# Seven half-size products in place of eight in the gated part, with wo converted early and q split as high, low, high

## The chip, the cores and the metric

The kernel runs on one core of a Trainium2 chip. The metric is device time in microseconds, from the runs of the whole kernel. TensorE (PE) multiplies into PSUM, ScalarE (ACT), VectorE (DVE) and GpSimd (POOL) do the elementwise work, and all DMAs are issued from SyncE's queue (SP).

## What is computed

Attention over 2 batches, 8 heads, 576 positions, head size 64, in which each row keeps its 32 largest scores; then a layer of four experts; then a gated layer, whose weights arrive as 64-bit floats. Cut to what matters:

```
attn = softmax(top32(q k^T / 8)) v              # (2,8,576,64) -> x (1152, 512)
for e in range(4):                              # D 512, F 1024
    out += p[:, e:e+1] * (relu(x @ w1[e]) @ w2[e])
x = out
a = x @ w_a                                     # 512 -> 1536
b = x @ w_b                                     # 512 -> 1536
return (a * b) @ w_out                          # 1536 -> 512
```

## The kernel before

Every product of the two layers is made of three matmuls: each 32-bit operand is kept as a high and a low part in the format fp32r, and high x high, high x low and low x high are added in PSUM. The 1152 tokens are nine tiles of 128, in groups of 1, 2, 3 and 3 tiles (`SIZES`). Group after group goes through attention and then through `experts` (`plain` for the first group, of one tile); a group's result is turned by TensorE and split into the high and low parts of `xs` in `replace`. The last stage is `gated`.

No order is written by hand. Each instruction, or short run of them, is added to a `Plan` with its engine, an expected duration (`dve`, `act`, `pool_`, `mm_r`), a key, what it waits for and the buffers it uses. `Plan.order` plays the engines forward in time with those durations and at each moment gives each engine the ready operation with the smallest key; `Plan.best` tries 42 variants and emits the best. The instructions then sit on each engine's queue in that fixed order. Operations marked `port=True` (DVE work from SBUF to SBUF) are not started in the plan while POOL works: `ok = not (op.port and free.get("POOL", 0.0) > now)`. Buffers are slots in regions of SBUF that are used again by later stages (`again`); a slot can be taken once all earlier users of its words are through. The names of the regions (`big`, `mid`, `low`, `raw`, `ys`) are the names that the trace shows.

The gated part runs over six steps of 256 of the 1536 inner columns. Each step converts 256 rows or columns of w_a, w_b and w_out in `d_unit` (two parts each of 512 KB of 64-bit data, 36 parts in all): per part one load, three ACT operations and seven DVE operations, which rebuild a 32-bit value and a remainder from the 64 bits and end in a high and a low part in `wd` (region `big`, five slots). Then for each half of 128 columns and each block of 384 tokens, `first` makes a and b (12 matmuls of 384 columns each, 4 pieces of the 512 times 3), ACT copies a out of PSUM, DVE multiplies it by b, ACT and DVE split the product into high and low (L1158, L1161, L1164, L1167). `second` multiplies with w_out: nine token tiles, six matmuls of 512 columns each, and DVE adds the result to `res` (L1179). `first`, `second` and `replace` of the early groups share three PSUM banks (`ms`); all matmuls have one line, L459, in `mm`, and all transposes L462.

Around it: `w_unit` loads and splits the experts' weights, the low part on POOL early and on DVE late (L894); `keys` and `start_pair` load and split k and q (L514 on ACT, L518 on POOL, L516 on DVE for the first pair); `masked` finds the top 32 on DVE (L728 MAX8, L736 MATCH_REPLACE).

## Time and profile before

| | us |
|---|---|
| runs of the whole kernel, median of 3 (lowest, highest) | 841.27 (840.20, 841.86) |
| the profiled execution's own time | 840.31 |
| its span, first to last instruction | 838.5 |
| PE busy | 809.1 |
| DVE busy | 702.3 |
| ACT busy | 535.8 |
| POOL busy | 266.4 |
| mean granted TensorE clock over the span | 0.984 |

Busy time is the union of an engine's instructions. Matmuls are pipelined: one of 384 columns shows a duration of 335 ns, but the next starts long before it ends, so the cost of one in a row is read from start to start. The 1.8 us between the span and the profiled time lie outside the instructions.

### The profile page before, as it was taken

How to read it: one execution, taken by the hardware profiler on the slowest of the kernel's cores; microseconds unless marked ns; L12 is line 12 of the kernel's file. 1: busy time of each engine (PE TensorE's matmuls, PEld its weight loads, DVE VectorE, ACT ScalarE, POOL GpSimd, SP SyncE). 2: the span in 40 equal slices, each digit the busy share in tenths (PEclk: the TensorE clock that was granted, in tenths of full speed). 3: DMA queues.
4: the chain of work that ended last, by engine and by line, in shares of the span. 5: the costliest groups of instructions: out<-in, count | busy, mean ns of one | idle time of the engine just before them, and what ended most of it. 6: DMA issues, size and time to landing. Idle time of an engine off the chain costs nothing.

```text
span 838.5 us, 13976 instructions
## 1 busy us (share of the span) xinstructions
PE 809.1 (96%) x5141; PEld 726.0 (87%) x5141; DVE 702.3 (84%) x1363; ACT 535.8 (64%) x965; POOL 266.4 (32%) x249
## 2 busy tenths in 40 slices
PE   7689999999999999999999999999999999999997
PEld 5477787889988899999999998999898989999896
DVE  7999999999999989999969998545235889899724
ACT  6888887999899798897756556343125535344220
POOL 4534433899898947764210000000000000000000
PEclk8699999999999999999999999999999999999999
DMA  6849967746644635432335657343002222323003
GB/s 185 278 132 299 331 216 232 235 137 204 203 137 153 184 115 153 130 104 99 101 124 178 201 161 217 125 126 101 1 1 64 88 77 74 101 79 98 26 1 113
DMA packets 83540, 117.05 MB, mean 140 GB/s; under 512 B 10640, under 2 KB 54672, under 8 KB 83472
## 3 DMA queue, kind: packets, MB, share of 16 engines
q1 hardware_dynamic: 83472, 116.17, 44.2%
q8 instruction: 40, 0.66, 0.3%
q14 instruction: 28, 0.23, 0.1%
HBM read 109.07 MB, written 7.08 MB: 139 GB/s over the span
## 4 chain that ended last, share of the span: by engine, by line
PE 64%; DVE 29%; ACT 3%; issue 2%; DMA 1%; POOL 1%; SPq 0%; POOLq 0%; ACTq 0%; DVEq 0%
PE ps L459 62%; DVE low L728 14%; DVE low L736 11%; PE ps L462 3%; DVE mid L967 1%; DVE ys L992 1%; DMA raw<-in_moe_w_dram 1%; ACT low L778 1%; ACT low L707 0%; ACT low L767 0%; ACT big L656 0%; POOL low L763 0%; DMA low<-in_q_dram 0%; DVE xs L872 0%; ACT mid L893 0%
## 5 line engine op out<-in xcount | busy, mean ns | idle before, releaser
L728 DVE MAX8 low<-low 128x8 f32<-128x576 f32 x288 | 204.4, 747 | 3.9 <-ACT low L707 3.6
L459 PE MATMUL ps<-xs,mid 128*128 128x384 f32 (+1 forms) x1152 | 203.3, 320 | 0.9 <-DVE mid L967 0.5
L459 PE MATMUL ps<-mid 128*128 128x512 f32 x768 | 198.1, 394 | 0.2
L459 PEld LDWEIGHTS ps<-xs,mid 128*128 128x128 f32 x1152 | 185.4, 189 | 9.9 <-DVE mid L967 0.9
L736 DVE MATCH_REPLACE8 low<-low 128x576 f32<-128x576 f32 x216 | 159.3, 743 | 0.0
L459 PEld LDWEIGHTS ps<-mid 128*128 128x128 f32 x768 | 139.7, 188 | 22.3 <-DVE mid L967 0.6
L459 PE MATMUL ps<-xs,big 128*128 128x384 f32 x864 | 152.3, 335 | 0.0
L459 PEld LDWEIGHTS ps<-xs,big 128*128 128x128 f32 x864 | 150.1, 188 | 1.3 <-DVE xs L1028 0.3
L893 ACT ACTIVATE mid<-raw 128x1024 fp32r<-128x1024 f32 x96 | 102.2, 1069 | 39.1 <-PE ps L459 29.2
L894 POOL TENSOR_TENSOR mid<-raw,mid 128x1024 fp32r<-128x1024 f32 x48 | 115.0, 2406 | 12.2 <-ACT mid L893 10.9
L763 POOL TENSOR_TENSOR low<-low 128x576 f32<-128x576 f32 x70 | 99.9, 1443 | 27.2 <-ACT low L759 26.8
L894 DVE TENSOR_TENSOR mid<-raw,mid 128x1024 fp32r<-128x1024 f32 x48 | 58.6, 1220 | 25.4 <-ACT mid L893 25.0
L963 ACT ACTIVATE mid<-ps 128x384 fp32r<-128x384 f32 (+1 forms) x96 | 44.2, 464 | 52.2 <-PE ps L459 49.3
L459 PE MATMUL ps<-big,mid 128*128 128x512 f32 x324 | 76.0, 391 | 0.0
L459 PEld LDWEIGHTS ps<-big,mid 128*128 128x128 f32 x324 | 60.4, 188 | 12.8 <-DVE low L1179 0.6
L967 DVE SCALAR_TENSOR_TENSOR mid<-ps,mid 128x384 fp32r<-128x384 f32 (+1 forms) x96 | 48.0, 504 | 23.8 <-ACT mid L963 23.4
L1158 ACT ACTIVATE low<-ps 128x384 f32<-128x384 f32 x36 | 17.7, 493 | 71.6 <-PE ps L459 71.4
L778 ACT ACTIVATE low<-low 128x576 f32<-128x576 f32 x70 | 51.5, 781 | 15.3 <-DVE low L775 15.2
L759 ACT ACTIVATE low<-low 128x576 f32<-128x576 f32 x70 | 52.5, 781 | 10.2 <-POOL low L753 10.1
L767 ACT ACTIVATE low<-low 128x576 f32<-128x576 f32 x70 | 54.9, 785 | 2.1 <-POOL low L763 2.1
L707 ACT ACTIVATE low<-ps 128x576 f32<-128x576 f32 x72 | 47.2, 660 | 9.7 <-POOL low L763 6.2
L462 PE MATMUL ps<-identr,low 128*128 128x128 f32 x324 | 47.3, 282 | 5.5 <-ACT low L778 4.4
(88 smaller groups left out, 1009.8 us busy)
## 6 DMA issues: line engine op xcount, KB each, us to landing
raw<-in_moe_w_dram SPq DMA_DIRECT2D x122, 512.0 KB, 3.7
big<-kscr SPq DMA_DIRECT2D x20, 576.0 KB, 5.5
low<-in_v_dram SPq DMA_DIRECT2D x24, 256.0 KB, 3.1
low<-in_moe_w_a_dram SPq DMA_DIRECT2D x12, 512.0 KB, 4.4
low<-in_moe_w_b_dram SPq DMA_DIRECT2D x12, 512.0 KB, 3.8
low<-in_moe_w_out_dram SPq DMA_DIRECT2D x12, 512.0 KB, 3.6
kscr<-big SPq DMA_DIRECT2D x8, 576.0 KB, 5.4
ys<-in_moe_w_dram SPq DMA_DIRECT2D x6, 512.0 KB, 5.6
```

The lines of the kernel that those rows point to most:

```text
L459: nc.tensor.matmul(out, l, r, **kw)
L462: nc.tensor.transpose(out, a, i)
L707: S, lambda: nc.scalar.activation(s.ap.rearrange("p (c n) -> p c n", c=2), at.ap[:, :, 0:HALF], AF.Copy),
L728: 62 + 1.04 * width, lambda at=at, cs=cs: nc.vector.max(m8v()[:, x, cs], at()), key + 0.02 * r, [done],
L736: lambda at=at, cs=cs: nc.vector.match_replace(out=src[1](), in_to_replace=m8v()[:, x, cs], in_values=at(), imm_value=LOW),
L759: S, lambda x=x, s=s: nc.scalar.activation(ev(x), s.ap, AF.Relu, bias=endv()[:, x, 1:2], scale=-STEEP),
L763: pool_(S), lambda x=x, s=s: nc.gpsimd.tensor_tensor(ev(x), s.ap, ev(x), op=ALU.subtract), ks, [a], [s, ep]
L767: lambda x=x: nc.scalar.activation(ev(x), ev(x), AF.Exp, bias=endv()[:, x, 0:1], scale=scale, accum_out=sums.ap[:, x:x + 1]),
L778: S, lambda x=x: nc.scalar.activation(ev(x), ev(x), AF.Copy, scale=sums.ap[:, x:x + 1]),
L893: hi = scalar(1024, lambda: nc.scalar.activation(u.ap[:, 0:1024], r.ap, AF.Copy), 500 + s, [ld], [u, r], sbuf=True)
L894: sub = lambda eng: eng.tensor_tensor(u.ap[:, 1024:2048], r.ap, u.ap[:, 0:1024], op=ALU.subtract)
L967: lambda h=h, p=p: nc.vector.scalar_tensor_tensor(h.ap[:, n:2 * n], p.ap[:, 0:n], 0.0, h.ap[:, 0:n], op0=ALU.max, op1=ALU.subtract),
```

## The change

**Strassen.** The two products of the gated part, x w_a and x w_b, are taken together as one product of a 2 x 2 block matrix x (two halves of the tokens, two halves of the 512) with a 2 x 2 block matrix (two halves of the 512; b and a). Seven products of half-size blocks replace eight, with sums of blocks as operands. The token halves are cut so that set 0 (`own` 0) pairs tokens 0 to 383 with 384 to 767, and set 1 (`own` 1) pairs 768 to 959 with 960 to 1151: a product has 384 columns in set 0 and 192 in set 1, and is made of 6 matmuls (2 pieces of the 256 times 3). `combine` takes the place of `replace` for the last two groups and also makes the sums of x (S1 to S4), in `xt`; for group 2 mostly on POOL, for the last group on DVE and ACT. `d_unit` now makes, for 128 inner columns, the full 32-bit values of w_b and w_a, the sums T1 to T4 of their halves, and high and low parts of all seven operands: 12 units in 3 slots of 3584 words (5 of 2048 before), behind 2 slots `vv` for the values before the split. `multiply` runs the seven products into six PSUM banks of their own (`pps`), builds the four blocks with one ACT copy and seven DVE additions from PSUM, multiplies a by b on POOL (two), splits on ACT (high) and POOL (low). `second` gets two banks of its own (`ns`).

**wo.** `narrow` converts w_out in six steps of 256 rows ahead of the gated part, with the same seven DVE operations per part as before, and writes the result to DRAM (`wscr`, 1 MB per step); `gated` loads it back, 1 MB per step, into one slot `uo`. Keys: `turn_of` gives two units, the six steps of w_out and the other ten units, in this order, keys from 1210 on, behind all weights of the experts.

**q.** q's block is stored as high, low, high (3 x 64) instead of high, high, low, low (4 x 64); the two transposes take columns 0 to 127 and 64 to 191. The sum of products is the same; the low part is now computed for 64 columns per tile and head instead of 128.

The regions are moved: `s` and `pt` get a region of their own, in which `xt` comes later; `ys` moves into `low`; `res` takes the space of the experts' raw weights.

```diff
+    wscr = dr.tile([F2 // 256, 128, 2048], F32, name="wscr")
...
-    qspls = big.slots("qspl", 1, 2 * 3 * 4 * D)
+    qspls = big.slots("qspl", 1, 2 * 3 * 3 * D)
...
-    wds = big.slots("wd", 5, 2048)
+    wds = big.slots("wd", 3, 2 * 7 * 256)
...
+    vvs = low.slots("vv", 2, 2048)
+    tps = [low.slots("tpa", 1, 4 * 384), low.slots("tpb", 2, 4 * 192)]
+    uos = mid.slots("uo", 1, 2048)
...
+    pps = banks("pp", [(i, i + 1) for i in range(6)], 2)
+    ns = banks("n", [(6, 7), (7, 8)], 2)
...
+    def split2(dst, src, m, key, after, tiles, eng):
...
+        sub = lambda e: e.tensor_tensor(dst()[:, :, 1], src(), dst()[:, :, 0], op=ALU.subtract)
...
-                        tr(p[:, i, lh], sqv()[:, j, i, lh].rearrange("p a d -> p (a d)"), identr)
+                        tr(p[:, i, lh], sqv()[:, j, i, lh:lh + 2].rearrange("p a d -> p (a d)"), identr)
...
+    sets = [(0, 384, 384), (768, 960, 192)]
...
+    def combine(c, y, yd):
+
+        own = c == len(GROUPS) - 1
...
+        def half(a):
...
+            s1 = vector(dve(n), lambda: nc.vector.tensor_tensor(tv(3), qv(), tv(1), op=ALU.add), K, f + [qo], [q_, tp])
+            s3 = pool(n, lambda e: e.tensor_tensor(tv(1), tv(1), tv(0), op=ALU.subtract), K, [s1], [tp])
+            s2 = pool(n, lambda e: e.tensor_tensor(tv(0), tv(3), tv(0), op=ALU.subtract), K, [s3], [tp])
+            if own:
+                s4 = vector(dve(n), lambda: nc.vector.tensor_tensor(tv(2), q_.ap[:, 0:n], tv(0), op=ALU.subtract), K, [s2], [q_, tp])
+            else:
+                s4 = pool(n, lambda e: e.tensor_tensor(tv(2), tv(2), tv(0), op=ALU.subtract), K, [s2], [tp])
...
+            h2 = scalar(3 * n, lambda: nc.scalar.activation(xv(0)[:, :, a], t3(), AF.Copy), K, [s4], [tp, xt], sbuf=True)
+            l2 = pool(3 * n, lambda e: e.tensor_tensor(xv(1)[:, :, a], t3(), xv(0)[:, :, a], op=ALU.subtract), K, [h2], [tp, xt])
...
+        for a in range(2):
+            half(a)
...
+    def turn_of():
+        taken.append(0)
+        return BASE + 10 * len(taken)
...
+    def narrow(f):
+
+        s = turn_of()
+        u, vv = wds.tile(), vvs.tile()
...
+                d, r, o4, o5, o7 = double(wo[r0:r0 + 128], s, t, vv, 1, False)
+                o8 = scalar(512, lambda: nc.scalar.activation(hi(), t(), AF.Copy), s, [o4], [vv, u], sbuf=True)
+                o9 = vector(dve(512), lambda: nc.vector.tensor_tensor(t(), t(), hi(), op=ALU.subtract), s, [o8, o5], [vv, u], port=True)
+                o10 = vector(dve(512), lambda: nc.vector.tensor_tensor(lo(), t(), r(), op=ALU.add), s, [o9, o7], [vv, d, u], port=True)
...
+        return load(lambda: wscr[f], lambda: u.ap[:, 0:2048].bitcast(F32), s, got, [u], 1 << 20)
...
+    def d_unit(f):
+
+        s = turn_of()
+        u, vv = wds.tile(), vvs.tile()
+        f0 = 2 * f * 128
...
+        for i, w in ((0, wb), (1, wa)):
+            src = w[:, f0:f0 + 256].rearrange("(a p) n -> p a n", p=128)
+            vs.append(double(src, s + 0.01 * i, lambda i=i: t(i), vv, 2, True))
...
+        t13 = vector(dve(512), lambda: nc.vector.tensor_tensor(
+            two(v(4, 2)), v(0).unsqueeze(1).to_broadcast([128, 2, 256]), two(v(1, 2)), op=ALU.subtract), s, vs, [vv], port=True)
+        t2 = vector(dve(256), lambda: nc.vector.tensor_tensor(v(6), v(2), v(4), op=ALU.subtract), s, [t13], [vv], port=True)
+        t4 = vector(dve(256), lambda: nc.vector.tensor_tensor(v(7), v(3), v(6), op=ALU.subtract), s, [t2], [vv], port=True)
+        got = []
+        for i, n, after in ((0, 3, vs), (3, 4, [t13, t4])):
+            hi = scalar(n * 256, lambda i=i, n=n: nc.scalar.activation(u.ap[:, i * 256:(i + n) * 256], v(i + 1, n), AF.Copy), s, after, [vv, u], sbuf=True)
+            got += [hi, vector(dve(n * 256), lambda i=i, n=n: nc.vector.tensor_tensor(
+                u.ap[:, (7 + i) * 256:(7 + i + n) * 256], v(i + 1, n), u.ap[:, i * 256:(i + n) * 256], op=ALU.subtract), s, [hi], [vv, u], port=True)]
...
+        units = [d_unit(f) for f in range(FRONT)]
+        kept_wo = [narrow(f) for f in range(F2 // 256)]
+        units += [d_unit(f) for f in range(FRONT, F2 // 128)]
...
+        def product(un, own, x, w_):
+            u, ud, uv = un
+            m = sets[own][2]
+            p = pps.tile()
+
+            def emit():
+                for a in range(2):
+                    for i, (l, r) in enumerate(((0, 0), (0, 1), (1, 0))):
+                        mm(p.ap[:, 0:m], uv(l, w_, a), operand(x, own, r, a), start=(a == 0 and i == 0), stop=(a == 1 and i == 2))
+
+            return p, tensor(6 * mm_r(m), emit, 1000 + nxt(), ud + xdone2[own], [p, u, late_x[0]])
+
+        def multiply(un, own, g):
+
+            m = sets[own][2]
...
+            p1, p6, p7, p5, p2, p3, p4 = [
+                product(un, own, x, w_)
+                for x, w_ in ((A11, B11), (S2, T2), (S3, T3), (S1, T1), (A12, B21), (S4, B22), (A22, T4))
+            ]
+            e1 = scalar(m, lambda: nc.scalar.activation(tv(0), p1[0].ap[:, 0:m], AF.Copy), K, [p1[1]], [p1[0], tp])
+            u2 = add(1, p6, 0, [e1])
+            u3 = add(2, p7, 1, [u2])
+            u4 = add(1, p5, 1, [u3])
+            c22 = add(3, p5, 2, [u3])
+            c11 = add(0, p2, 0, [u2])
+            c12 = add(1, p3, 1, [u4])
+            c21 = add(2, p4, 2, [c22])
+            g0 = mul(0, 0, 1, [c11, c12])
+            g1 = mul(1, 2, 3, [c21, g0])
+            cs = slice(sets[own][0], sets[own][0] + 2 * m)
+            hi = scalar(2 * m, lambda: nc.scalar.activation(g.ap[:, 0:n][:, cs], tv(0, 2), AF.Copy), K, [g0, g1], [g, tp], sbuf=True)
+            lo = gpsimd(pool_(2 * m), lambda: nc.gpsimd.tensor_tensor(
+                g.ap[:, n:2 * n][:, cs], tv(0, 2), g.ap[:, 0:n][:, cs], op=ALU.subtract), K, [hi], [g, tp])
+            return [hi, lo]
...
+            both = [(units[2 * f + part], gs_.tile()) for part in range(2)]
+            gd = {}
+            for own, part in ((0, 0), (0, 1), (1, 0), (1, 1)) if pending else ((0, 0), (1, 0), (0, 1), (1, 1)):
+                gd[own, part] = multiply(both[part][0], own, both[part][1])
+                if pending:
+                    pending.pop()()
...
+                p, o = second(gts, [un_o + (0,), un_o + (1,)], t * 128, (), ns.tile())
```

The sums of blocks in `d_unit` and `combine` are as shown; `double` holds the first six DVE operations and two ACT operations of the old `d_unit`, with one more DVE addition of the remainder for w_a and w_b.

## Rows read from the trace of the kernel before

**Rows 1.** The page: busy time by engine, then tenths in 40 slices.
```profile
PE 809.1 (96%) x5141; PEld 726.0 (87%) x5141; DVE 702.3 (84%) x1363; ACT 535.8 (64%) x965; POOL 266.4 (32%) x249
...
DVE  7999999999999989999969998545235889899724
...
PEclk8699999999999999999999999999999999999999
```

**Rows 2.** Chain that ended last, in order of time: start, length, what.
```profile
479.32 137.13 PE ps L459 x696
...
617.95 215.94 PE ps L459 x1139
```

**Rows 3.** Windows: length, then busy PE, PEld, DVE, ACT, POOL, clock, DMA.
```profile
50.00:440.00 390.00, 381.57 (x2874) 334.52 (x2874) 379.65 (x795) 332.40 (x608) 241.84 (x207) 1.00 0.55 175
...
440.00:607.90 167.90, 167.90 (x881) 152.83 (x876) 116.35 (x175) 78.44 (x118) 0.00 (x0) 1.00 0.45 139
607.90:821.40 213.50, 213.49 (x1147) 201.49 (x1147) 153.64 (x284) 85.12 (x158) 0.00 (x0) 1.00 0.20 60
```

**Rows 4.** Timeline of PE, gated part: start, length, instructions merged.
```profile
647.35 24.11 PE L459 MATMUL ps<-xs,big 128*128 128x384 f32 x138
671.29 0.86 PE L459 MATMUL ps<-big,mid 128*128 128x512 f32 x3
...
672.52 11.95 PE L459 MATMUL ps<-big,mid 128*128 128x512 f32 x51
684.31 15.96 PE L459 MATMUL ps<-xs,big 128*128 128x384 f32 x91
```

**Rows 5.** Timeline of PE, an experts' stretch with 256 columns.
```profile
229.73 1.58 PE L459 MATMUL ps<-xs,mid 128*128 128x256 f32 x12
231.15 0.86 PE L459 MATMUL ps<-mid 128*128 128x512 f32 x3
```

**Rows 6.** Timeline of PE, an attention stretch with transposes of 128 columns.
```profile
189.12 0.63 PE L462 MATMUL ps<-identr,big 128*128 128x128 f32 x6
189.58 0.59 PE L459 MATMUL ps<-xs,mid 128*128 128x256 f32 x3
```

**Rows 7.** Groups by line and shape: count, busy us, mean ns, idle before.
```profile
L894 POOL TENSOR_TENSOR mid<-raw,mid 128x1024 fp32r<-128x1024 f32 x48 | 115.0, 2406 | 12.2 <-ACT mid L893 10.9 <-POOL low L772 0.6 <-POOL big L518 0.3
...
L894 DVE TENSOR_TENSOR mid<-raw,mid 128x1024 fp32r<-128x1024 f32 x48 | 58.6, 1220 | 25.4 <-ACT mid L893 25.0 <-PE ps L459 0.4
...
L1179 DVE TENSOR_TENSOR low<-ps,low 128x512 f32<-128x512 f32 x45 | 30.1, 686 | 11.6 <-PE ps L459 11.4
...
L1120 DVE SCALAR_TENSOR_TENSOR low<-low 128x512 uint32<-128x512 uint32 x36 | 24.8, 689 | 0.8
...
L1161 DVE TENSOR_TENSOR low<-ps,low 128x384 f32<-128x384 f32 x36 | 20.0, 555 | 36.3 <-ACT low L1158 30.3 <-PE ps L459 3.4 <-PE ps L462 2.5
...
L1118 DVE TENSOR_SCALAR low<-low 128x512 uint32<-128x512 uint32 x36 | 15.3, 424 | 0.8
...
L967 DVE SCALAR_TENSOR_TENSOR mid<-ps,mid 128x256 fp32r<-128x256 f32 x32 | 12.9, 412 | 0.0
...
L518 POOL TENSOR_TENSOR big<-low,big 128x384 fp32r<-128x384 f32 x8 | 7.9, 1011 | 3.0 <-ACT big L514 1.8 <-DMA raw<-in_moe_w_dram 1.2
```

**Rows 8.** Timeline of DVE: two instructions that follow each other, merged.
```profile
498.36 1.01 DVE L967 SCALAR_TENSOR_TENSOR mid<-ps,mid 128x384 fp32r<-128x384 f32 x2
```

**Rows 9.** Timeline of POOL: the same two instructions at two places.
```profile
393.93 2.80 POOL L763 TENSOR_TENSOR low<-low 128x576 f32<-128x576 f32 x2 [0.89 <-ACT low L759]
...
409.06 3.45 POOL L763 TENSOR_TENSOR low<-low 128x576 f32<-128x576 f32 x2 [1.81 <-ACT low L759]
```

**Rows 10.** Timeline of DVE at the second of these places.
```profile
408.62 1.20 DVE L894 TENSOR_TENSOR mid<-raw,mid 128x1024 fp32r<-128x1024 f32 x1
```

**Rows 11.** Writes into the wd slots before the gated part: count, ns, first and last start.
```profile
L1129 DVE TENSOR_TENSOR big<-low x10: 680/683/693, 446.4 to 514.4; 128x512 fp32r<-128x512 f32 x10
```

**Rows 12.** DMA issues: line, count, KB each, us to landing.
```profile
kscr<-big SPq DMA_DIRECT2D x8, 576.0 KB, 5.4
```

More of the change, by code (lines that the diff above doesn't have):

```diff
@@ L40, in __init__ @@
         self.name, self.aps, self.region, self.spans = name, aps, region, spans
+        self.whole = False
         self.free = set(range(len(aps)))
@@ L65, in cells @@
         a, b = self.spans[i]
-        return [(o.name, j) for o in self.beside for j, (c, d) in enumerate(o.spans) if c < b and a < d]
+        return [(o.name, j) for o in self.beside for j, (c, d) in enumerate(o.spans) if c < b and a < d or self.whole and o.rank < self.rank]
     @property
@@ L78, in ap @@
     def ap(self):
-        return self.slots.aps[self.slot]
+        a = self.slots.aps[self.slot]
+        return a[0][a[1]] if isinstance(a, tuple) else a
 class Op:
@@ L209, in place @@
                         continue
+                    if s.whole and o.rank < s.rank:
+                        break
                     if any(a0 < b1 and b0 < a1 for b0, b1 in o.spans):
@@ L327 @@
 URGENT = 3
+BASE, FRONT = 1200, 2
 def body(tc, q, k, v, probs, w1, w2, wa, wb, wo, out):
@@ L350, in body, with __init__, __getitem__ @@
     dr = stack.enter_context(tc.tile_pool(name="dr", bufs=1, space=DRAM))
+    class Again:
+        def __init__(self, region, dtype):
+            self.region, self.dtype, self.t = region, dtype, None
+        def __getitem__(self, span):
+            if self.t is None:
+                r = self.region
+                self.t = sb.tile([128, r.words], self.dtype, name=r.name + "_again", tag=r.name)
+            return self.t[:, span[0]:span[1]]
     class Region:
@@ L356, in __init__, with again @@
             self.t = sb.tile([128, words], dtype, name=name, tag=name)
-            self.name, self.words, self.at, self.rank = name, words, 0, 0
-        def again(self):
+            self.name, self.words, self.at, self.rank, self.other = name, words, 0, 0, None
+        def again(self, dtype=None):
             self.at, self.rank = 0, self.rank + 1
+            self.other = Again(self, dtype) if dtype else None
         def slots(self, name, n, words):
@@ L365, in slots @@
             assert self.at <= self.words, (name, self.at, self.words)
-            s = Slots(name, [self.t[:, a:b] for a, b in spans], self.name, spans)
-            s.rank = self.rank
+            s = Slots(name, [(self.other, ab) if self.other else self.t[:, ab[0]:ab[1]] for ab in spans], self.name, spans)
+            s.rank, s.whole = self.rank, self.other is not None
             return s
@@ L397, in body @@
     wraws = raw.slots("wraw", 4, 1024)
-    low = Region("low", 12300 + 4 * 1152 - 3 * 640, F32)
+    first_ = Region("lowa", 4 * 2 * S + 4 * S, F32)
+    pts = first_.slots("pt", 4, 2 * S)
+    ss = first_.slots("s", 4, S)
+    low = Region("low", 9228 + 3 * DM, F32)
     kraws = low.slots("kraw", 2, 2 * M4 * D)
@@ L518, in split @@
             b = gpsimd(pool_(n), lambda: nc.gpsimd.tensor_tensor(dst_lo(), src(), dst_hi(), op=ALU.subtract), key, [a], tiles)
+        return [a, b]
+    def split2(dst, src, m, key, after, tiles, eng):
+        a = scalar(
+            m * 2 * D, lambda: nc.scalar.activation(dst()[:, :, ::2], src().unsqueeze(2).to_broadcast([128, m, 2, D]), AF.Copy),
+            key, after, tiles, sbuf=True,
+        )
+        sub = lambda e: e.tensor_tensor(dst()[:, :, 1], src(), dst()[:, :, 0], op=ALU.subtract)
+        if eng == "DVE":
+            b = vector(dve(m * D) + 30, lambda: sub(nc.vector), key, [a], tiles, port=True)
+        else:
+            b = gpsimd(pool_(m * D), lambda: sub(nc.gpsimd), key, [a], tiles)
         return [a, b]
@@ L623, in start_pair @@
         for j in range(2):
[L624 to L625 removed]
+            sp[j] += split2(lambda j=j: sqv()[:, j, 0:m], lambda j=j: rqv()[:, j], m, key + 0.03 + (0.004 * j if n == 0 else 0), lds, [rq, sq], eng)
             if m < T:
@@ L1134, in gated @@
     def gated():
[L1136 removed]
+        res = [ress[t // 8].tile() for t in range(NT)]
         n = 128 * NT
         rd = {}
[L1139 to L1171 removed]
@@ new lines, in gated @@
+        for f in range(F2 // 256):
+            uo = uos.tile()
+            ld = load(lambda uo=uo: uo.ap.bitcast(F32), lambda f=f: wscr[f], 705 + seq[0], [kept_wo[f]], [uo], 1 << 20)
+            un_o = uo, [ld], lambda i, uo=uo: uo.ap[:, i * 1024:(i + 1) * 1024].rearrange("p (a n) -> p a n", a=2)
+            gts = []
+            both = [(units[2 * f + part], gs_.tile()) for part in range(2)]
[4 more added lines that the diff above has]
+                    pending.pop()()
+            for part, (_, g) in enumerate(both):
+                gts.append((g, [gd[0, part], gd[0, part], gd[1, part]], n))
```

228 lines of the change are left out of this document (130 added, 98 removed).

## The prediction

> **What bounds the kernel now.** I began with the page's busy shares. PE is at 96% of the span, and its slices read 9 from early on with a full clock; DVE reads 9 up to the middle and again in the gated part [rows 1]. So two engines can be the bound, and the stage decides. The chain of waits in order of time ends in 137 us and 216 us of nothing but PE matmuls, with one run of transposes between [rows 2]: from about 440 us on no other engine ends a wait that matters. The windows confirm it: between 440 and 607.9 us PE is busy for 167.9 of 167.9 us and DVE for 116.4; in the gated part, 607.9 to 821.4, PE for 213.5 of 213.5 and DVE for 153.6. POOL does nothing after 440. Before 440, PE has gaps of 8.4 us in 390 and DVE of 10.4 [rows 3]. What the change saves on PE in the gated part therefore comes off the end, if DVE and POOL keep up with it.
>
> **PE.** In the gated part 138 matmuls of 384 columns take 671.29 - 647.35 = 23.94 us, 173.5 ns each, and 51 of 512 columns 684.31 - 672.52 = 11.79 us, 231 ns each [rows 4]. The sum fits: 864 x 0.1735 + 270 x 0.231 + 1.2 for the transposes = 213.5 us, the whole window. 256 columns cost (231.15 - 229.73) / 12 = 118 ns [rows 5]. At 2.4 GHz columns alone would be 160 and 106.7 ns, so the fixed part is 12 to 13.5 ns. No row shows 192 columns. From the nearest rows it is 80 + 13.5 = 93.5 ns. From below it is 80 + 12 = 92; from above I take the transposes, 128 columns in (189.58 - 189.12) / 6 = 77 ns [rows 6], a fixed part of 24, so 104.
>
> The change removes 864 matmuls of 384 columns, 149.9 us. It adds 12 units x 7 products x 6 = 504 of 384 columns (87.4 us) and 504 of 192 (47.1 us; 46.4 to 52.4). Gain 15.4 us, with ends 10.1 and 16.1. Seconds and transposes stay as they are. Break-even would be at 124 ns for 192 columns, more than 256 columns cost here.
>
> **The start of the gated part.** With `combine` of the last group pending, both set 0 products go first: 84 matmuls, 14.6 us. The second of them wants the one `tpa` slot, which the first holds until its low part: an addition (0.56), two POOL multiplications (1.01 each), ACT's high part, and POOL's low part of 768 elements, which I put at 1.85 between 384 at 1.01 and 1024 at 2.41 [rows 7]. Meanwhile only the three banks of `ms` are free, worth 3 x 1.04 us of products, and the transposes, 1.2 us; the chain is some 5 to 6 us with its waits. Then set 1 waits for `combine`, some 7 us of DVE work behind the transposes. Nothing else is there for PE. I take 2 us lost, with 0 and 5 as ends. At the last step the same chain of set 0 faces 42 x 93.5 ns = 3.9 us of set 1 products: 0.6 us lost, since nothing follows but the seconds that wait for it.
>
> **DVE, unit by unit.** One conversion part before is 3 instructions of 0.424 and 4 of 0.69, 4.03 us. A unit now has two doubles of 3 x 0.424 + 3 x 0.69 = 3.34, sums of 0.69 + 2 x 0.42 (as 256 elements at 0.412) and low parts of 768 and 1024 elements, 0.95 + 1.22: 10.4 us in 17 instructions. The additions from PSUM are 7 x 0.555 for set 0 and 7 x 0.34 for set 1 (by the line through 256 and 384 columns): 6.3 us. Half a step's second additions are 4.5 x 0.686 = 3.1 us [rows 7]. That is 19.8 us per unit against 11.2 + 6.2 = 17.4 us of PE. Instructions that follow each other overlap: two of 0.55 take 1.01 [rows 8], 0.09 less. In the window of before the durations of its DVE work sum to 171 us in 284 instructions, full overlap would leave 145, measured are 153.6 [rows 3]: a third of the overlap is lost.
>
> Some of this is done ahead. Five old units, ten parts, were converted from 446 to 514 us [rows 11]. From 440 to 607.9 DVE idles 51.5 us [rows 3] and these ten parts give back 40.3: 91.8 us. Asked of it now: w_out's 12 parts, 48.4, three units, 31.1, and the values of two more, 13.4: 92.9 by durations in some 160 instructions, 83 with the overlap as measured. It fits, barely. w_out's 1 MB writes pass through one slot; 576 KB land in 5.4 us [rows 12], so 1 MB in perhaps 9.6, six times conversion and write 90 to 106 us, over by 590. Each load back has 22 us of products to hide in. Without that cover it costs 9.6 us a step.
>
> In the gated part the last unit's first product comes 5 x 34.9 + 11.2 = 186 us after the start. (A unit's products are 42 x (173.5 + 93.5) ns = 11.2 us, a step 2 x 11.2 + 12.5 = 34.9.) By then DVE owes 9 x 10.4 - 13.4 for units, 11 x 6.3 for additions, 24.7 for second additions and 7 for `combine`: 181 us by durations in some 340 instructions, 181 - 0.67 x 340 x 0.09 = 160 with the overlap as measured. Alone it fits.
>
> **POOL beside DVE.** POOL comes back: per unit 2 x 1.01 + 1.85 for set 0 and 2 x 0.59 + 1.01 for set 1, 6.1 us, 67 us before that last unit [rows 7]. The trace shows what it meets. Two POOL instructions of 576 elements take 2.80 us at 393.93 and 3.45 at 409.06 [rows 9], and at the second place DVE had begun an instruction with both inputs in SBUF at 408.62 that ran until 409.82 [rows 10]: POOL's began to run when it was through. The plan also starts no `port` operation of DVE while POOL works. So conversions and POOL take turns; only additions from PSUM run beside POOL, and these with the second additions fill 94 of 186 us, half. If POOL falls at random, 33 us of its 67 leave DVE nothing to do: 160 + 33 = 193 of 186. If it always lies beside additions: 160. I take the middle, 176, because finished banks wait in PSUM and can be kept for POOL's time. It fits, with 1.5 us for single waits.
>
> The Trainium skill, SBUF — State Buffer, section "Who interferes with whom", says that a DVE instruction with two SBUF inputs and a GpSimd instruction that reads SBUF contend for one port pair, held for a whole instruction, while one with at most one SBUF input, outside the two-port modes, does not contend. The trace agrees for POOL behind DVE (0.65 us); DVE behind POOL no row shows. By that rule alone the sum would be the random case or worse, as in the first rival.
>
> **q and the regions.** q's low parts shrink to half on POOL, the largest from 1.01 to about 0.6, some 10 us of POOL in all. POOL was at 62% up to 440 us, DVE at 97% [rows 3], and DVE's top 32 is untouched, so I take 0; the most it can give is part of PE's 8.4 us of gaps, 3 us. `combine` for group 2, some 17 us of POOL, lies under the experts.
>
> **Sum,** against the profiled execution's 840.3: -15.4 (PE) + 2.0 + 0.6 + 1.5 = 829.0. The runs' median lies 1.0 above it, so I say 830 for the median.
>
> **The rivals.**
>
> *DVE and POOL taking turns become the bound: slower.* Place: conversions of units 4 to 12. For it: 19.8 us by durations against 17.4, and rows where POOL waits. Against it: DVE idled 60 us in the window of before and the work ahead fits. Each us over 186 is a us lost; the gain of 11.3 is gone when 160 + x = 186 + 11.3, x = 37 of POOL's 67 us without cover. At 50 us the time is 829 + 24 = 853, at all 67 it is 870. Chance 0.21.
>
> *The same, partly:* 28 to 36 us without cover, or work ahead that falls short by a unit (10 us, of which the slack of 10 in the middle case takes most). Time 832 to 839. Chance 0.20.
>
> *It cancels:* 839 to 842.5. Chance 0.10.
>
> *Small matmuls are dear:* 104 ns instead of 93.5, 5.3 us more: 835. For it the transposes; against it 256 and 512 columns on one line. Chance 0.05.
>
> *q's split closes PE's gaps too:* 3 us less, 827 or below. Chance 0.06.
>
> My forecast, PE-bound with small waits, 826 to 833, has the remaining 0.38 and is the likeliest.
>
> **The numbers.** A measurement of this kernel can tell about 0.2%, 1.7 us. Faster: 0.38 + 0.20 + 0.05 + 0.06 = 0.69; within: 0.10; slower: 0.21. The range leaves out about 1 in 10 on each side: low 823, which is the bound of 92 ns and part of q's gain (829 - 0.7 - 3, less some of the 4 us of waits); high 848, half of the slower rival. Where PE stays the bound, the range is 824 to 835.
>
> **What would show it.** Right: 504 matmuls of 384 and 504 of 192 columns in the gated part, the latter 92 to 104 ns from start to start; PE full but for about 2 us near 620 and 0.6 us before the last seconds; from the first gated product to the last matmul some 215 us, where it was 213.5 + 54 x 0.231 = 226; DVE at 86 to 95% there and POOL at a third; the clock at its upper level of 2.4 GHz, as in every slice of before in which PE reads 9 [rows 1]. Wrong: PE waiting in every step for the low part of a unit on DVE or of `g` on POOL, POOL instructions of 1.85 us that take 2.5 and more, or conversions of units still running when their products are due. Units fewer than three ready at 608 us would say that the work ahead failed.

## The result and the profile after

The changed kernel takes 847.26 us in the median (846.03 to 848.22), the kernel before, beside it, 841.18 (840.20 to 841.86): a ratio of 1.0078, 95% interval 1.0065 to 1.0090. It is slower by 6.1 us, little but clear of the noise, where I forecast 11 us less than before. The profiled execution took 847.36 us.

The page of the kernel after: busy time by engine, then tenths in 40 slices.
```profile
PE 809.6 (96%) x5285; PEld 720.0 (85%) x5285; DVE 771.4 (91%) x1507; ACT 537.3 (64%) x951; POOL 364.8 (43%) x335
...
DVE  7989999999899999999976989998898988989973
...
PEclk9699999999999999999999999999999999999999
```
PE's busy time is what it was before [rows 1], 809 us, although 864 matmuls of 384 columns became 504 of 384 and 504 of 192. DVE is fuller by 69 us and POOL by 98. The clock is no part of it: from the third slice on it reads 9 in both, and 1.00 in the windows below, its upper level of 2.4 GHz.

Windows of the kernel after, from 440 us to shortly before the first gated products (612.8), and from there into the last seconds (the matmuls of `second`, a product with w_out): length, then busy PE, PEld, DVE, ACT, POOL, clock, DMA.
```profile
440.00:610.60 170.60, 169.34 (x923) 152.81 (x923) 148.31 (x226) 98.71 (x147) 20.16 (x13) 1.00 0.63 201
610.60:831.00 220.40, 218.22 (x1324) 201.89 (x1323) 196.18 (x385) 72.65 (x121) 84.95 (x72) 1.00 0.22 71
```
PE is still the engine that is full in the gated part, as in [rows 3]. So for the most part the gain did not go into waits of PE: PE's own work did not shrink.

Timeline of PE in the kernel after: a step's products, and the last 54 seconds at the end of the kernel.
```profile
661.12 2.05 PE L487 MATMUL ps<-xs,big 128*128 128x384 f32 x12
663.01 1.50 PE L487 MATMUL ps<-lowa_again,big 128*128 128x192 f32 x12
664.35 1.50 PE L487 MATMUL ps<-xs,big 128*128 128x192 f32 x12
665.70 0.92 PE L487 MATMUL ps<-lowa_again,big 128*128 128x192 f32 x6
...
826.75 14.11 PE L487 MATMUL ps<-mid 128*128 128x512 f32 x54
```
Twelve matmuls of 192 columns take 664.35 - 663.01 = 1.34 us and the next twelve 1.35: 112 ns from start to start. Over all 504, each counted to the next start, the median is 111 ns and the mean, with what waits there are, 111.5. The forecast had 93.5 with 104 as its end. The last 54 seconds take 14.11 us, where 231 ns each [rows 4] gave 12.5.

Adding up starts in both traces, the gated part's matmuls (products, its seconds and its transposes) take 226.2 us after and 225.6 before; all before them 611.8 and 605.5. My sum had 225.6 - 15.4 + 2.0 + 0.6 + 1.5 = 214.3 for the first and no change for the second. So 11.9 us have to be found in the gated part and 6.3 ahead of it. Against the kernel before, the gated part is 0.7 us longer and the stages ahead of it 6.3: nearly all of the slowdown itself lies ahead.

### The profile page after: what moved, and what is told of

Its sections match the earlier page's. It is cut to its first block, busy times and chain, and to the rows that moved or that the text cites. A ratio compares the mean times of both kernels' runs of the same rounds, so it can differ in the third digit from the quotient of the medians.

```text
span 845.6 us, 14637 instructions
## 1 busy us (share of the span) xinstructions
PE 809.6 (96%) x5285; PEld 720.0 (85%) x5285; DVE 771.4 (91%) x1507; ACT 537.3 (64%) x951; POOL 364.8 (43%) x335
## 4 chain that ended last, share of the span: by engine, by line
PE 60%; DVE 22%; ACT 9%; POOL 5%; issue 3%; DMA 1%; POOLq 0%; DVEq 0%; ACTq 0%
PE ps L487 57%; DVE low L767 7%; DVE low L775 6%; PE ps L490 3%; ACT low L806 1%; POOL mid L933 1%; ACT low L817 1%; ACT mid L932 1%; ACT lowa L746 1%; DVE mid L933 1%; DVE big L1269 1%; ACT low L798 1%; DVE raw L1360 1%; ACT lowa L875 1%; POOL low L802 1%
## 5 line engine op out<-in xcount | busy, mean ns | idle before, releaser
L487 PE MATMUL ps<-mid 128*128 128x512 f32 x1092 | 282.2, 397 | 4.0 <-POOL mid L933 2.1
L487 PEld LDWEIGHTS ps<-mid 128*128 128x128 f32 x1092 | 199.3, 189 | 43.5 <-DVE raw L1360 4.0
L802 POOL TENSOR_TENSOR low<-lowa,low 128x576 f32<-128x576 f32 x70 | 101.3, 1462 | 31.1 <-ACT low L798 31.0
L775 DVE MATCH_REPLACE8 low<-low 128x576 f32<-128x576 f32 x144 | 106.3, 745 | 0.0
L487 PE MATMUL ps<-xs,big 128*128 128x384 f32 (+1 forms) x576 | 93.3, 307 | 1.8 <-ACT low L1324 1.7
L487 PEld LDWEIGHTS ps<-xs,big 128*128 128x128 f32 x576 | 85.5, 190 | 4.9 <-ACT low L1324 2.0
L1315 DVE TENSOR_TENSOR low<-ps,low 128x384 f32<-128x384 f32 (+1 forms) x168 | 71.8, 449 | 17.0 <-PE ps L487 15.7
L487 PE MATMUL ps<-lowa_again,big 128*128 128x384 f32 (+1 forms) x432 | 70.8, 305 | 0.0
L487 PEld LDWEIGHTS ps<-lowa_again,big 128*128 128x128 f32 x432 | 64.4, 190 | 1.4
L798 ACT ACTIVATE low<-lowa,low 128x576 f32<-128x576 f32 x70 | 53.3, 782 | 12.7 <-POOL low L792 12.6
```

Source lines behind the costliest of these rows:

```text
L487: nc.tensor.matmul(out, l, r, **kw)
L775: lambda at=at, cs=cs: nc.vector.match_replace(out=src[1](), in_to_replace=m8v()[:, x, cs], in_values=at(), imm_value=LOW),
L798: S, lambda x=x, s=s: nc.scalar.activation(ev(x), s.ap, AF.Relu, bias=endv()[:, x, 1:2], scale=-STEEP),
L802: pool_(S), lambda x=x, s=s: nc.gpsimd.tensor_tensor(ev(x), s.ap, ev(x), op=ALU.subtract), ks, [a], [s, ep]
L1315: return vector(dve(m), lambda: nc.vector.tensor_tensor(tv(out), p.ap[:, 0:m], tv(i), op=ALU.add), K, [o] + after, [p, tp])
```

## The experiments

Ratios are to the kernel before, measured beside it, with 95% intervals. The times of stages come from one execution of each kernel, and two executions of the same order can differ by some 2 us: experiment 1, with the order of the kernel after and narrower matmuls, shows 228.2 us in the gated part and 611.0 ahead of it. Experiments 4 to 10 and 13 to 15 emit an order that was planned anew; 1, 2, 3, 11 and 12 keep the order that they are compared with.

**1. Narrower products in set 1.** The products of set 1 multiply only 128 of their 192 columns; the rest of each result is left out. The order is the same.

```diff
-                        mm(p.ap[:, 0:m], uv(l, w_, a), operand(x, own, r, a), ...)
+                        mm(p.ap[:, 0:128 if own else m], uv(l, w_, a), operand(x, own, r, a)[:, 0:128 if own else m], ...)
```


> The changed kernel with the products of set 1 cut from 192 to 128 columns and nothing else altered, the order on every engine included (a third of set 1's columns is left out). Theory 1, a matmul with 128 columns of weights cannot follow the one before it in less than about 110 ns, however few columns it has: start to start stays at 109 to 112 ns, where the 192 columns now show 111, and the time stays at 847 within 1.5 us. Theory 2, the 111 ns are 80 ns of columns and 31 of fixed cost: start to start falls by 27 ns to 84, PE has 504 x 0.027 = 13.4 us less to do, and the time falls to 834 to 840. Theory 3, DVE and POOL bound the stage: start to start falls as in theory 2, but PE waits instead and the time falls by less than 3 us.

847.29 us, ratio 1.0086 [1.0071, 1.0101]: nothing is gained. Timeline of PE in this kernel:
```profile
663.91 1.50 PE L487 MATMUL ps<-lowa_again,big 128*128 128x128 f32 x12
665.25 1.50 PE L487 MATMUL ps<-xs,big 128*128 128x128 f32 x12
666.62 0.89 PE L487 MATMUL ps<-lowa_again,big 128*128 128x128 f32 x6
```
1.34 us for twelve again. A third fewer columns cost the same, so these matmuls are held by a floor of 111 ns, the same for 128 and for 192 columns. The trace of before has no product of this kind below 256 columns. Its narrow matmuls in a row are of other kinds. Timeline of PE, kernel before:
```profile
148.60 1.13 PE L459 MATMUL ps<-xf,ys 128*128 128x128 f32 x8
149.49 0.71 PE L462 MATMUL ps<-identr,big 128*128 128x128 f32 x6
...
152.66 1.02 PE L459 MATMUL ps<-raw,low 128*128 128x512 f32 x2
```
Eight matmuls of 128 columns take 0.89 us, 111 ns each, the very number. But they are the first group's, which `plain` multiplies as plain 32-bit numbers and not as fp32r, and in that format the two of 512 columns at 152.66 start some 430 ns apart, a quarter of which is 107 ns. So this row fits a dearer column and says nothing of a floor. The transposes from which I took my upper end [rows 6] ran at 77 ns; they were the wrong neighbours too, a different operation that isn't held by the same floor. The Trainium skill, TensorE: Matmul & The Clock Gate, section "LDWEIGHTS (loading the stationary operand)", puts a load at the stationary operand's columns divided by 1.2; by that an estimate for 128 columns is 107 ns, and the measured 111 agrees with a loop held by its loads. That the loads are the cause was not tried by itself, and the transposes speak against it as the whole cause: each of them has a load of 128 x 128 in the trace as well, and they followed each other in 77 ns.

**2. q alone.** The kernel before with only q as high, low, high, in its old order.

```diff
-                        tr(p[:, i, lh], sqv()[:, j, i, lh].rearrange("p a d -> p (a d)"), identr)
+                        tr(p[:, i, lh], sqv()[:, j, i, lh:lh + 2].rearrange("p a d -> p (a d)"), identr)
```


> The kernel before with q stored as high, low, high alone, its plan's durations kept so that the order is that of before. Theory 1 (q is hidden under DVE's top 32): within 1.5 us of the kernel before. Theory 2 (q's split is what holds the attention stage up in the changed kernel, which comes to the gated part 6 us later): 2 to 6 us slower than before. Theory 3 (POOL's shorter work closes PE's gaps): 1.5 to 3 us faster.

841.12 us, ratio 1.0004 [0.9994, 1.0014]. In the kernel before, q neither gives nor takes.

**3. POOL cut in the gated part.** The kernel after in the same order, with the two multiplications and the low part on POOL done for 16 columns only (the rest of a x b and its low part is left out).

```diff
-    nc.gpsimd.tensor_tensor(tv(out), tv(i), tv(j), op=ALU.mult)
+    nc.gpsimd.tensor_tensor(tv(out)[:, 0:16], tv(i)[:, 0:16], tv(j)[:, 0:16], op=ALU.mult)
```


> The changed kernel with POOL's three instructions of each product set in the gated part cut to 16 columns (the multiplication of a by b and the low part of the product are left out for the rest), in the same order. Theory 1 (the dear small matmuls have eaten the gain and POOL costs little): only the wait of 1.8 us at the start of the gated part and the short waits of the seconds go, 1 to 3 us faster than the changed kernel, 844 to 846. Theory 2 (DVE and POOL taking turns bound the stage, the rival of the prediction): 5 us and more faster, 842 or below.

844.56 us, ratio 1.0050 [1.0035, 1.0065]: 2.7 us less than the kernel after, 1.8 of them in the gated part, no more than executions differ by. POOL is not what holds the changed kernel.

**4. A third bank for the seconds.** Five banks for products and three for seconds.

```diff
-    pps = banks("pp", [(i, i + 1) for i in range(6)], 2)
-    ns = banks("n", [(6, 7), (7, 8)], 2)
+    pps = banks("pp", [(i, i + 1) for i in range(5)], 2)
+    ns = banks("n", [(5, 6), (6, 7), (7, 8)], 2)
```


> The changed kernel with three PSUM banks for the seconds and five for the products, where it has two and six. Theory 1 (two banks are too few for the seconds: 54 matmuls take 14.1 us at the end where they took 12.4 before): the last 54 matmuls take 12.4 to 12.6 us again and the time falls by 1.6 to 3 us. Theory 2 (DVE is late, not the banks few): the last seconds stay near 14 us. Theory 3 (five banks are too few for the products): new waits of PE inside the products, slower by 1 us or more.

844.18 us, ratio 1.0047 [1.0031, 1.0062]. The gated part falls by 3.3 us to 222.9. Timeline of PE, this kernel, its last seconds; then of DVE in the kernel after, at the same place:
```profile
823.56 12.45 PE L487 MATMUL ps<-mid 128*128 128x512 f32 x54
```
```profile
829.03 1.37 DVE L1360 TENSOR_TENSOR raw<-ps,raw 128x512 f32<-128x512 f32 x2 [1.73 <-PE ps L487]
```
With two banks the first matmul of a tile waited for DVE's addition two tiles back: in the kernel after DVE's addition of the first tile ends at 829.72 and the third tile's first matmul starts at 829.78, and so at every second tile. The change lowered the banks from three to two, and my sum had the seconds "stay as they are". Counted from start to start, all 324 seconds take 74.0 us in the kernel before, 76.7 after, 75.0 here, and 73.8 in experiment 9. So about half of the 3.3 us is the seconds'; the rest lies in the products and can be the other order or the execution.

**5 and 6. Other orders.** The kernel before, and the kernel after, each with other seeds for the plan's 42 variants; the work is the same.

```diff
-            draw = random.Random(r)
+            draw = random.Random(r + 1000)
```


> The kernel before with other random numbers in its plan, so that another of the possible orders is emitted; the work is the same. Theory 1 (the 6 us that the changed kernel loses before the gated part are, for some 4 us of the attention stage, the luck of the order): this kernel lies 1.5 to 5 us away from the kernel before, probably slower, all of it before 440 us. Theory 2 (orders are equal within noise, the change itself delays the attention stage): within 1.2 us of the kernel before.

> The changed kernel with other random numbers in its plan. Theory 1 (luck of the order): 1.5 to 4 us away from the changed kernel's 847, with another start of the gated part than 612.8 us. Theory 2 (the change itself delays what comes before the gated part): the gated part starts within 1.2 us of 612.8 and the time is 846 to 848.

844.26 us, ratio 1.0047 [1.0031, 1.0064] for the kernel before, with all of the loss ahead of the gated part (609.8 against 605.5); 851.80 us, ratio 1.0138 [1.0123, 1.0153] for the kernel after (615.6 against 611.8 ahead of it, 228.4 against 226.2 in it). One other draw for each, both slower: what an order happens to be is worth some 4 us in either kernel, most of it ahead of the gated part.

**7. The true price in the plan.** The plan counts 192 columns at 93.3 ns. Here it counts 111.

```diff
-    return max(n, 96) / 2.4 + 13.3
+    return max(n, 235) / 2.4 + 13.3
```


> The changed kernel whose plan counts a matmul of fewer than 235 columns at 111 ns, the duration that the trace shows, where it counted 93 for 192 columns. The work is the same. Theory 1 (the cost itself is lost and the order hardly matters): 845.5 to 848. Theory 2 (the plan's wrong cost makes other engines late in its order): 2 us and more faster than the changed kernel, 845 or below, the waits at the start of the gated part and in the seconds shorter.

852.48 us, ratio 1.0147 [1.0132, 1.0162]. Both theories missed: the stage before did not change much (611.2), but in the new order the gated part takes 231.6 us; in four of its six steps PE loses 1.2 to 2.7 us to waits. A truer price did not make a better order; whether that is more than an order's luck is open.

**8. `combine` of group 2 on DVE.**

```diff
-            if own:
+            if True:
                 return vector(dve(w), lambda: emit(nc.vector), key, after, tiles, port=True)
```


> The changed kernel with the sums of x for group 2 made on DVE, where POOL makes them beside DVE's splitting of weights from 483 to 506 us. Theory 1 (POOL and DVE take turns there, which delays the low parts of weights: PE waits 2.6 us between 490 and 512 us): these waits go, 1.5 to 3 us faster than the changed kernel. Theory 2 (DVE has no room for 9 us more): the conversions come later, PE waits elsewhere, same time or slower.

844.17 us, ratio 1.0044 [1.0029, 1.0059], 3 us better than the kernel after; ahead of the gated part 609.3 instead of 611.8. Windows from 480 to 520 us, and DVE's low parts of the experts' weights from 440 to 520, first after, then this kernel, then the window of experiment 4, which has another order than after and leaves these sums on POOL:
```profile
480.00:520.00 40.00, 38.74 (x199) 34.04 (x198) 35.67 (x46) 24.06 (x37) 20.08 (x12) 1.00 0.47 146
L933 DVE TENSOR_TENSOR mid<-raw,mid 128x1024 fp32r<-128x1024 f32 x18 | 26.1, 1452 | 3.1 <-ACT mid L932 3.1
```
```profile
480.00:520.00 40.00, 40.00 (x213) 36.84 (x212) 39.90 (x65) 27.06 (x41) 0.00 (x0) 1.00 0.58 188
L933 DVE TENSOR_TENSOR mid<-raw,mid 128x1024 fp32r<-128x1024 f32 x19 | 23.1, 1218 | 3.4 <-ACT mid L932 3.4
```
```profile
480.00:520.00 40.00, 38.75 (x197) 34.08 (x196) 35.66 (x47) 24.89 (x38) 20.08 (x12) 1.00 0.46 150
```
With POOL at work there, DVE begins 46 instructions in 40 us; without it 65, though they include POOL's sums. Timeline of DVE and of POOL at one place, kernel after:
```profile
491.08 2.48 DVE L933 TENSOR_TENSOR mid<-raw,mid 128x1024 fp32r<-128x1024 f32 x1 [0.39 <-ACT mid L932]
...
489.81 2.68 POOL L1105 TENSOR_TENSOR lowa_again<-low,lowa_again 128x1152 fp32r<-128x1152 f32 x1 [1.28 <-ACT lowa_again L1104]
```
POOL's instruction ends at 492.49. DVE's, which takes 1.22 us elsewhere, lasts until 493.56, 1.07 us after that: it waited for POOL. Three us could be the luck of the new order, but this loss comes and goes with POOL's work and not with the order: PE is busy for 38.7 of these 40 us in after, 3 and 4, and for all 40 in before, 8 and 9. At the median prices of before, PE's starts lose 2.6 us there in the first three and 0.1 in the others.

**9. Both repairs,** 4 and 8 together.

> The changed kernel with three banks for the seconds and five for the products, and with the sums of x for group 2 on DVE: the two edits that each took 3 us off. Theory 1 (two separate waits): both gains add up, 840 to 842, no difference from the kernel before. Theory 2 (one shared cause, or another order's luck): 843 to 846.

841.69 us, ratio 1.0012 [1.0003, 1.0021]: the gains add up. Gated part 223.7, ahead of it 608.8.

**10. Even halves.** As 9, with the token halves cut evenly: all 1008 products have 288 columns, above the floor (288 take 133 ns), and PE's price falls to 134.1 us for all products, what the forecast had (87.4 + 47.1 = 134.5). `combine` is written anew for it, all on DVE and ACT, and set 1 has one slot for its blocks where it had two.

```diff
-    sets = [(0, 384, 384), (768, 960, 192)]
+    sets = [(0, 288, 288), (576, 864, 288)]
```


> The kernel of the run before this one with the token halves cut evenly: both sets pair 288 tokens with 288, so that every product has 288 columns where set 0 had 384 and set 1 had 192. Theory 1 (a matmul costs the larger of about 110 ns and its columns with 13 ns): 133 ns from start to start, as the scores' matmuls of 288 columns show, 504 x (174 + 111 - 2 x 133.5) = 9 us less of PE; 6 to 10 us faster than that kernel, 830 to 836, and faster than the kernel before. Theory 2 (columns count alone, 31 ns fixed at small sizes): 288 columns cost 133 to 151 and the gain is 0 to 9 us. Theory 3 (DVE and POOL bound the stage): PE's matmuls get cheaper but PE waits, 0 to 4 us faster.

840.36 us, ratio 0.9996 [0.9987, 1.0005]. The matmuls cost what they should, 133 ns. Ahead of the gated part 604.7, but in it 225.6: the 9.5 us that PE's matmuls cost less than in 9 are all lost to waits there.

**11 and 12. What fills DVE then.** The kernel with even halves in the same order: once with POOL's three instructions cut to 16 columns as in 3; once with DVE's 45 additions of seconds cut to 16 columns (most of the output is left out).

> The kernel with even halves (288 and 288 columns), in the same order, with POOL's three instructions of each product step of the gated part (two multiplications and the low part) cut to 16 columns; their results are not the reference's. In the gated part of the uncut kernel DVE is busy 48 to 49 of each 50 us and PE waits some 12 us. Theory A (DVE's own instructions fill the stage, and POOL's 86 us there run beside them): the time stays within 2.5 us of the 840.4 of the uncut kernel. Theory B (DVE is full because it waits for POOL's turns, as the prediction's first rival had it): DVE's durations shrink (the 512-wide adds of the seconds, 680 ns, go below 640; the passes at the doubled weights below 560) and most of the 12 us go: 828 to 833.

> The kernel with even halves, in the same order, with the 45 DVE instructions that add the second products of steps 2 to 6 (128x512, 680 ns each) cut to 16 columns, so that some 27 us of DVE's 222 in the gated part go; the outputs are not the reference's. Both theories A and B (DVE bounds the stage once the first products cost 133 ns for 288 columns) say that the gated part falls from 225.6 us to PE's own work, 1008 matmuls at 133 ns and 324 at 230 ns, or 208.6 us, with some 3 to 5 us of single waits: 827 to 830. If instead the waits of PE come from the order of the plan or from single late results, not from DVE's load, the time stays above 835.

828.00 us, ratio 0.9854 [0.9839, 0.9869], and 836.82 us, ratio 0.9960 [0.9946, 0.9974]. Windows from 640 to 800 us of the even kernel, of the one with POOL cut, and of the one with DVE cut:
```profile
640.00:800.00 160.00, 156.30 (x955) 140.66 (x954) 157.74 (x290) 56.09 (x90) 61.56 (x52) 1.00 0.24 77
```
```profile
640.00:800.00 160.00, 160.00 (x1024) 149.77 (x1023) 149.69 (x306) 56.37 (x91) 19.72 (x56) 1.00 0.24 81
```
```profile
640.00:800.00 160.00, 157.24 (x976) 143.87 (x975) 146.49 (x296) 56.08 (x91) 63.42 (x52) 1.00 0.25 81
```
With POOL cut, PE has no gap in these 160 us, begins 1024 matmuls where it began 955, and the gated part falls from 225.6 to 213.1 us. So it is POOL's work that costs, as theory B had it, though its sign in the additions of the seconds failed (680 ns with POOL, 688 without). Taking about 23 us of DVE's own work away (45 additions from 0.68 to 0.17 us) gives 2.8, and PE still has gaps while DVE is idle for 13.5 of the 160 us. Both theories had 827 to 830 here; 836.8 lies where the expectation put waits that come from the order or from single late results, and not from DVE's load. So the sum of DVE's work isn't the bound; it matters which of its instructions are late.

POOL can make results late by holding up DVE, or because the next set and the seconds wait for POOL's own results. For the first, 10 and 11 give DVE the same instructions in the same order, which can be compared one by one: from 606 to 826 us the 177 that read only SBUF take 24.4 us more in all with POOL at work, the 217 that read PSUM 0.6 less. For the second there is less: of the 24 copies by ACT with which a set starts to build its blocks two waited for POOL's low part, PE 1.43 us behind the first of them, and PE waited for POOL itself once, 0.97 us. How the 12.4 us divide between the two was not counted. Timeline of POOL, DVE and PE, even kernel, at one place of the first kind:
```profile
744.42 1.43 POOL L1350 TENSOR_TENSOR mid<-low,mid 128x576 fp32r<-128x576 f32 x1 [1.07 <-ACT mid L1349]
```
```profile
744.08 0.45 DVE L1329 TENSOR_TENSOR low<-ps,low 128x288 f32<-128x288 f32 x1
744.45 2.48 DVE L1283 TENSOR_TENSOR big<-low,big 128x1024 fp32r<-128x1024 f32 x1
746.85 1.90 DVE L1329 TENSOR_TENSOR low<-ps,low 128x288 f32<-128x288 f32 x5
```
```profile
747.35 1.06 PE L487 MATMUL ps<-xs,big 128*128 128x288 f32 x6 [0.90 <-DVE low L1329]
```
POOL begins 0.03 us before DVE's low part, which then takes 2.48 us instead of 1.22 and ends 1.08 us after POOL's end; five additions from PSUM stand behind it in DVE's queue, and PE waits 0.90 us for the first of them. The 168 additions of the products from PSUM do not slow down (439 to 460 ns each with POOL at work, 440 to 459 with POOL cut). The Trainium skill, SBUF — State Buffer, section "Who interferes with whom", says both of these: a DVE instruction with two SBUF inputs contends with POOL's reads, one with a single SBUF input, outside the two-port modes, does not, and who comes first holds the ports for its whole instruction.

**13 to 15. Work from POOL to DVE.** The even kernel with the low part, with both multiplications, and with one of them on DVE. The second one's edit:

```diff
-    return gpsimd(pool_(m), lambda: nc.gpsimd.tensor_tensor(tv(out), tv(i), tv(j), op=ALU.mult), K, after, [tp])
+    return vector(dve(m), lambda: nc.vector.tensor_tensor(tv(out), tv(i), tv(j), op=ALU.mult), K, after, [tp], port=True)
```


> Even halves with the low part of the gated values (24 subtractions of 576 columns) moved from POOL to DVE, which takes the order's plan along (the plan orders anew, worth some 4 us either way). POOL loses 34 of its 84 us in the gated part, DVE gains 24 x 0.7 = 17 us of its own. Theory of turns: with POOL's work cut, DVE was busy 198 us from 600 to 826; that and 17 and 0.147 us (12.4 / 84) for each of POOL's remaining 50 us is 222: the gated part falls from 225.6 to about 222 and the time to 835 to 839. Theory of DVE's own load: 17 us more on the bound, 850 or more.

> Even halves with both multiplications of each product step (48 of 288 columns) moved from POOL to DVE; the order is planned anew. POOL loses 48 us, DVE gains 48 x 0.34 = 16. Theory of turns: 198 + 16 + 0.147 x 34 = 219 us for DVE, so the gated part falls to 219 to 221 and the time to 833 to 837. Theory of DVE's own load: 849 or more.

> Even halves with one of the two multiplications (24 of 288 columns) moved from POOL to DVE; the order is planned anew. Theory of turns: 198 + 8 + 0.147 x 60 = 215 us for DVE, at PE's 213 with POOL cut, so the gated part falls to about 218 and the time to 831 to 836. Theory of DVE's own load: 844 or more.

| moved to DVE | us | ratio | gated part | ahead of it |
|---|---|---|---|---|
| nothing (10) | 840.36 | 0.9996 [0.9987, 1.0005] | 225.6 | 604.7 |
| low part | 842.95 | 1.0034 [1.0023, 1.0046] | 223.3 | 609.5 |
| both multiplications | 836.17 | 0.9947 [0.9927, 0.9968] | 217.3 | 611.8 |
| one multiplication | 842.11 | 1.0015 [1.0005, 1.0024] | 221.0 | 611.6 |

The gated parts are shorter than in 10 and lie within 3 us of the numbers of the theory of turns; the theory of DVE's own load, which had them rise, is out. Its ranking failed: it had one multiplication best, and both together are, by 3.7 us. The fall of 2.3 for the low part is within what an order or an execution is worth; that of 8.3 is more than any other order made there (5.4, experiment 7). The times missed upwards in the first and third, because each kernel is planned anew and the part ahead of the gated one came out 5 to 7 us worse than in 10. The second is the one version with all of its work that beats both kernels. Of the kernel with both on DVE, windows from 640 to 800 us and DVE's multiplications from 650 on:
```profile
640.00:800.00 160.00, 159.84 (x1007) 147.44 (x1007) 156.13 (x330) 56.28 (x91) 27.33 (x18) 1.00 0.23 74
...
L1332 DVE TENSOR_TENSOR low<-low 128x288 f32<-128x288 f32 x34 | 15.2, 447 | 0.0
```
A multiplication takes DVE 0.45 us and took POOL 1.00 in 10. PE is full again in this stretch; its one long wait, 3.9 us, is at the start of the gated part.

## Why the prediction was wrong

**The price of 192 columns, the step that took most of the gain.** I drew a line through 256 and 512 columns to 93.5 ns, and closed the range at 104 from transposes. Measured are 111.5 in the mean: 504 x (111.5 - 93.5) ns = 9.1 us of the 15.4 (experiment 1). The trace of before had no matmul of this kind below 256 columns, so nothing held that line at its lower end. My rival "small matmuls are dear" named the right place with half the price and a chance of 0.05. With the right price the sum would still have been 2.2 us below the time before; the direction was turned by the next two steps, 2.7 and 2.5 us, and by 3.8 us that stay open.

**"Seconds stay as they are".** They went from 74.0 to 76.7 us with two banks in place of three (experiment 4), 2.7 us that the sum had at nothing. The 504 products of 384 columns take 92.2 us, where my sum had 87.4 and 2.0, 0.6 and 1.5 for the start, the last step and single waits: 0.7 more. So these waits were about right in sum, and 9.1, 2.7 and 0.7 make the 11.9 by which the gated part missed my 214.3 to within 0.6. The largest wait at the start is the one that I had placed near 620. PE at the start of the gated part, kernel after:
```profile
627.88 1.32 PE L487 MATMUL ps<-xs,big 128*128 128x384 f32 x6 [1.66 <-ACT low L1324]
```
ACT, the same:
```profile
627.34 0.49 ACT L1324 ACTIVATE low<-ps 128x384 f32<-128x384 f32 x1 [0.41 <-POOL mid L1336]
```
ACT's copy, the first to write into `tpa`, waited for POOL's low part of the set before, which is the chain that I had drawn.

**"`combine` for group 2 lies under the experts".** It took POOL at a time when POOL had been idle, and DVE's splitting of weights, which that stage needs, waited for it: 2.5 of the 6.3 us ahead of the gated part (experiment 8), which the sum had at nothing. The remaining 3.8 have the size of an order's luck (5 and 6), and experiment 10, with the same attention and `combine` on DVE, came to 604.7 ahead of the gated part, where the kernel before has 605.5. That luck is all they are is likely and was not shown, since an order can't be drawn for one kernel from the other.

**POOL beside DVE.** I put its turns at a middle value that fits "with 1.5 us for single waits". At the price that I forecast for PE, POOL's work costs 12.4 us (experiments 10 and 11), most likely through DVE: the place that the first rival named, with its chance of 0.21, though not its size, since 840.4 is the time of "it cancels". The rival's sum over all of DVE's work was not the way either: 23 us less of it gave 2.8 (experiment 12). In the changed kernel POOL costs 1.8 us in the gated part. That PE at 111 ns was slow enough for DVE to keep up would explain the difference and was not tried by itself. Experiment 10 has the matmuls at the forecast's price and not the forecast's time, so a right price alone would hardly have given 830.

**What held:** PE is the full engine in the gated part; w_out's way through DRAM costs nothing that shows (1 MB lands in 4.7 to 5.5 us on the page of after, where I had estimated 9.6); units are ready in time; q is neutral; the clock stays up. The direction was wrong. That the time lies inside the range is luck: its upper end was drawn for POOL's turns, which cost 1.8 us in the gated part of this kernel.

## What to carry to other kernels

Before halving a matmul's width, look in the trace for matmuls as narrow as the new ones, in the same number format, with the same size of weights, in a row; a line through wide ones says nothing of a floor below them, and neither do transposes or another format. If there are none, a run with the columns cut, like experiment 1, shows the price. Here it was 111 ns for 128 and 192 columns alike, so halves are better cut evenly than 384 and 192; the even cut alone gave nothing (experiment 10), and the gated part fell only when POOL's work was cut or its multiplications moved as well. When an engine has an idle partner, count what the partner's instructions do to single instructions of the first, and what stands behind those, not only the sum of work: two multiplications that take POOL 1.00 us each and DVE 0.45 were better on DVE, although DVE was the busier one. And where a program plans the order, a change of 1% can't be read from the total alone; split the time by stage, and run the old kernel in other orders to learn what luck is worth.

## What the runs showed of the hardware

- Matmuls in a row with weights of 128 x 128 (fp32r): 111 ns for 128 (experiment 1) and for 192 columns, 120 for 256, 133 for 288, 174 for 384, 229 for 512 (medians from start to start). From 256 up that is columns / 2.4 plus 13 to 16 ns; drawn down, this line meets 111 ns at an estimated 230 columns. What makes the floor, and why some transposes of the same size run at 77 ns, is open.
- DVE with two SBUF inputs waits for POOL's instruction when POOL was first, even by 0.03 us (1.22 to 2.48 us); DVE with one input in PSUM does not (439 to 460 ns). In experiments 10 and 11, 58 us less of POOL's busy time (84.0 against 25.5 from 606 to 826 us) made DVE's instructions that read only SBUF 24.4 us shorter in all, and the time 12.4 us.
